# One packing product placed earlier, and h's tiles moved to one place modulo 512 bytes

## The chip, the core and the metric

The kernel runs on one core of a Trainium2 chip. The core has a matrix engine (TensorE, PE in the profile), a vector engine (VectorE, DVE), a scalar engine (ScalarE, ACT), GpSimd (POOL) and a queue for transfers (SyncE, SP). Data lies in SBUF, 128 partitions wide; PE writes its results to PSUM, in eight buffers of 2 KB a partition. A matmul on PE has two instructions: a load of the stationary operand (PEld in the profile) and the matmul that streams the moving operand.

The metric is the time of one execution on the device, in microseconds.

## What is computed

Eight batches, each with eight heads, 576 positions and a head size of 64, go through a two-step attention over 32 "pack" queries; all outputs, 4608 rows of 512, go through a gated feed-forward layer.

```
scale = 1.0 / np.sqrt(64)
def sm_attn(qq, kk, vv):
    s = scale * qq @ kk.T
    a = exp(s - max(s))
    a = a / (sum(a) + 1e-09)
    return a @ vv
p_packed = sm_attn(p, k, v)               # 32 rows a head
x = sm_attn(q, p_packed, p_packed)        # 576 rows a head
x = x.transpose(0, 2, 1, 3).reshape(4608, 512)
g = x @ w_gate                            # 512 x 1536
out = (silu(g) * (x @ w_val)) @ w_out     # 1536 x 512
```

## The kernel before

The kernel never forms x. For each batch it multiplies the packed values into the gate and value weights (the **middle product**, tiles mh and ml, `m_mm`, L570 to L588), so that the gate and value matmuls take the second attention's weights a2 directly. Operands of the large matmuls are split into a high and a low part (mh and ml, a2h and a2l, hh and hl, wo_h and wo_l), of which three products are summed.

Batch 0 and the loading of the weights follow a list of words written out by hand (PROGRAM, L41). Batches 1 to 7 run through `batch` (L903): a loop over twelve chunks `fc` of 128 hidden columns. Each chunk has two halves, A (256 positions) and B (320). Each half does

- `gv_chunk` (L623): twelve matmuls, six for the gate and six for the value, into two PSUM buffers named gv (two exist, used in turns); ACT takes silu of the gate into sg (L644), DVE multiplies it with the value into hf (L648) and, in half B, a rest into t (L651);
- `h_split` (L614): ACT writes hh, the high part of hf (L177), DVE writes hl, the rest (L618);
- six matmuls of the chunk before (`out_mm`, L654): the stationary operand is hl or hh, the moving one is wo_h or wo_l, the sum goes to one of four PSUM buffers named acc.

So on PE the halves alternate: gate and value matmuls of this half, then the output matmuls of the chunk before.

The attention of the next batches is done in pieces between these matmuls. Two tables, FIRST (for batch 2) and LATER (for the later ones), give each piece a place: `4.ha turn1` is chunk 4 of the batch before, half A, at the point between the writing of hh and that of hl; `hb` is the same point of half B, `a` and `b` the points just behind silu, and numbers count the points in the matmuls. What is issued at such a point stands in each engine's program there, and each engine works its own program in order. Here the pieces of interest are

- `turn0`, `turn1` (`q_turn`, L459): for half of the heads each, DVE scales the exponentials e by the factors and transposes them into a (L464, L467);
- `pack` (`q_pack`, L471): 80 small matmuls with a as the stationary and the values v_t as the moving operand, into one gv buffer (L479), then a transpose by DVE into ppt (L485). Each small matmul is in float32 and appears as two matmuls and two loads in the profile: 160 and 160. This is called the packing product below.

In LATER, the second transpose stands at `4.ha`, the packing product at `5.ha`. In chunk 5, half A, the middle product of chunk 6 (L266, eight matmuls in the program, 16 in the profile) comes directly ahead of it.

Tiles come from pools that give each name a fixed number of buffers in turns, laid one behind the other in SBUF. The tiles hh and hl (`h_tile`, L608) have three buffers of 280 elements of four bytes; of these, 256 are used, starting at an element that changes with each use:

```
n = places[t] = places.get(t, -1) + 1
at = (0, 1, 2, 4, 8, 12, 16, 20)[n % 8]
return pool.tile([P, 280], F32R, tag=t, bufs=3, name=t)[:, at : at + 256]
```

The middle product's tiles mh and ml are shifted in the same way (L576). All of w_out's tiles start at the same byte modulo 512 of a partition.

Of the kernel before, what the change touches and what calls it, by code (L numbers as in the profile page):

```python
# [10 lines left out]
F32 = mybir.dt.float32  # L11
F32R = mybir.dt.float32r
# [8 lines left out]
B, H, S, D = 8, 8, 576, 64  # L21
NP = 32
DM, DF = 512, 1536
P = 128
NPAR, NHP = 2, 4
NFC = DF // P
NSC = -(-S // P)
NJ, SQ = 4, S // 4
# [7 lines left out]
F64_HI_LEAST = float(np.array(897 << 20, np.int32).view(np.float32))  # L36
F64_HI_MOST = float(np.array(0x47EFFFFF, np.int32).view(np.float32))
SPLIT = 5
LOW_WORD = -(2.0**-51) * 15 / 16

PROGRAM = """  # L41
# [23 lines left out]
FIRST = """  # L65
# [33 lines left out]
LATER = """  # L99
# [32 lines left out]
def tile_pack_attention_swiglu(ctx: ExitStack, tc: tile.TileContext, qT, kT, v, vq, pT, wgv, wout, out):  # L132
# [5 lines left out]
    pool = ctx.enter_context(tc.tile_pool(name="pool", bufs=1))  # L138
# [51 lines left out]
    def f64_convert(dst, st, shape):  # L190
# [5 lines left out]
        yield nc.scalar.activation(dst, hi.bitcast(F32), AF.Abs)  # L196
        yield nc.scalar.activation(lo.bitcast(F32), lo.bitcast(U32), AF.Identity, bias=minus_two, scale=LOW_WORD)
        yield nc.vector.tensor_scalar(dst, dst, F64_HI_LEAST, F64_HI_MOST, op0=ALU.max, op1=ALU.min)
# [11 lines left out]
    def pair(dtype, name):  # L210

        return pool.tile([P, 2, DM], dtype, tag="pair", bufs=NFC + 1, name=name)
# [11 lines left out]
    def wout_high(fc):  # L224
        k, i = divmod(fc, 2)
        if i == 0:
            wo_h[k], wo_l[k] = pair(F32R, "wo_h"), pair(F32R, "wo_l")
        pin(nc.scalar.copy(wo_h[k][:, i], wos[k][:, i]))
# [126 lines left out]
        nc.vector.reciprocal(rs[:, 2], rs[:, 1])  # L355

    def s1_scale(b):
        pp = pool.tile([P, NPAR, D], F32, tag="pp", bufs=1, name="pp")
        nc.vector.tensor_tensor(
            pp,  # L360
            pps[b][0][:, : NPAR * D].rearrange("p (r d) -> p r d", r=NPAR),
            st1[b][2][:, 2].unsqueeze(2).broadcast_to([P, NPAR, D]),
            op=ALU.mult,
        )
        pps[b].append(pp)
# [57 lines left out]

    def q_gather(b):

        x = pool.tile([P, NJ, 2, H], F32, tag="x1", bufs=1, name="x1")
        zd = dram.tile([P, 2, H], F32, tag="zd", bufs=2, name="zd")
        nc.sync.dma_start(zd, sq[b][1].rearrange("p s r h -> p s (r h)"))
        for i in range(NJ):
            nc.sync.dma_start(x[NP * i : NP * i + NP], zd.rearrange("(j n) s h -> n j s h", j=NJ))  # L430
        sq[b].append(x)
# [168 lines left out]
    def m_part(b, k, fcs):  # L600
        m_mm(b, k, fcs)
        m_high(b, k, fcs)

    t4 = {}

    places = {}

    def h_tile(t):  # L608

        n = places[t] = places.get(t, -1) + 1  # L610
        at = (0, 1, 2, 4, 8, 12, 16, 20)[n % 8]
        return pool.tile([P, 280], F32R, tag=t, bufs=3, name=t)[:, at : at + 256]

    def h_split(src, hi, lo, between=lambda: False, tag=""):  # L614
        hh, hl = (pool.tile([P, 256], F32R, tag=t + tag, bufs=2, name=t) if tag else h_tile(t) for t in ("hh", "hl"))
        copy(hi, hh, src)
        last = between()
        low = lo.tensor_tensor(hl, src, hh.bitcast(F32), op=ALU.subtract)  # L618
        if last:
            pin(low)  # L620
        return hh, hl
# [32 lines left out]
    def out_mm(acc, hh, hl, c, fc):  # L654
        for i, (h_, w_) in enumerate(((hl, wo_h), (hh, wo_l), (hh, wo_h))):
            nc.tensor.matmul(  # L656
                acc[:, :],
                h_[:, c : c + P],
                w_[fc // 2][:, fc % 2],
                start=(fc == 0 and i == 0),  # L660
                stop=(fc == NFC - 1 and i == 2),
            )

    def emit_out(acc, row, eng):
# [13 lines left out]
        "q1r": lambda d: q_read(d, 1, (0, 1)),  # L678
        "q1e": lambda d: q_exp(d, 1),
        "q1z": lambda d: (q_sums(d, 1), q_gather(d)),  # L680
        "common": q_common,
        "common_e": q_common_exp,
# [10 lines left out]
    for i in range(2):  # L693
        for name, f in (
# [8 lines left out]
        ):  # L703
            words2[f"{name}{i}"] = (lambda f, i: lambda d: f(d, (d + i) % 2))(f, i)

    def plan_of(b):

        plan = {}
        for d in (b + 1, b + 2):
            if d >= B:  # L710
                continue
            for line in (FIRST if d == 2 else LATER).strip().splitlines():
                place, *todo = line.split()
                fc, place = place.split(".")
                fc = int(fc) + NFC * (d - b - 1)
                if (0 if d > 2 else -NFC) <= fc < NFC:
                    plan.setdefault((fc, int(place) if place.isdigit() else place), []).extend((words2[w], d) for w in todo)
        return lambda fc, place: bool([f(d) for f, d in plan.pop((fc, place), ())])

    with tc.manual_schedule(engines={mybir.EngineType.PE}):  # L720
# [17 lines left out]
        with tc.manual_schedule(  # L738
# [25 lines left out]

            h0 = [pair(F32, "h0") for _ in range(SPLIT)]
            for k in (*range(NFC // 2 - 2), NFC // 2 - 1, NFC // 2 - 2):
# [24 lines left out]
            def half(i):  # L791
                fc, is_b = order[i]
                if fc // 2 < SPLIT:
                    return h0[fc // 2][:, fc % 2, 256 * is_b : 256 * is_b + 256]
# [18 lines left out]
            def h_high(i):  # L813
                hs[i].append(h_tile("hh"))
                nc.scalar.copy(hs[i][1], hs[i][0])

            def h_low(i):
                hs[i].append(h_tile("hl"))
                nc.vector.tensor_tensor(hs[i][2], hs[i][0], hs[i][1].bitcast(F32), op=ALU.subtract)

            def outs(i):
                fc, is_b = order[i]
                for c in range(2):
                    if fc // 2 >= SPLIT:
                        out_mm(accs[2 * is_b + c], *hs[i][1:], c * P, fc)
# [29 lines left out]
            def half_of(f, b):  # L855
# [9 lines left out]
                "z_top": lambda x: s1_top(0), "z_exp": lambda x: s1_exp(0, True), "z_turn": lambda x: s1_turn(0, x),  # L865
                "z_turned": lambda x: s1_turned(0, x, nc.vector), "z_pack": lambda x: s1_pack(0),
                "z_sums": lambda x: s1_sums(0, True), "z_scale": lambda x: s1_scale(0), "z_flip": lambda x: s1_flip(0),
                "z_ppt": lambda x: s1_ppt(0), "two_mm": lambda c: (None if c else s2_tiles(0), s2_mm(0, c)),
                "two_block": lambda c: s2_block(0, c), "narrow": narrow, "heat": warm_up,
# [5 lines left out]
                "s1_keep": lambda x: s1_keep(1, x), "s1_top": lambda x: s1_top(1), "s1_exp": lambda x: s1_exp(1),  # L875
                "s1_turn": lambda x: s1_turn(1, x), "s1_turned": lambda x: s1_turned(1, x, nc.scalar),
                "s1_pack": lambda x: s1_pack(1), "s1_sums": lambda x: (s1_sums(1), s1_scale(1)),
                "s1_flip": lambda x: s1_flip(1), "s1_ppt": lambda x: s1_ppt(1),
                "s2_mm": two_mm, "s2_block": lambda x: s2_block(1, x), "s2_max": half_of(s2_max, 1),
# [7 lines left out]
            for word in PROGRAM.split():  # L887
                name = word[: word.index(":") + 1] if ":" in word else word.rstrip("0123456789")
# [14 lines left out]
        def batch(b, behind):  # L903
            if not b % 2:
                t4_of(b)
            run = plan_of(b)
            ha, hb = {}, {}
            accs, rows = [], []
# [7 lines left out]
            for fc in range(NFC):  # L916
                count = [0]

                def fill():
                    count[0] += 1  # L920
                    if count[0] == 2:
# [3 lines left out]
                        elif fc % 2 and fc + 1 < NFC:  # L925
                            m_part(b, (fc + 1) // 2, both)
                    if b == 1 and 1 <= fc <= 2 * SPLIT - 4 and count[0] == 7:
                        wout_high(fc + 3)
# [91 lines left out]
```

## Time and profile before

| | us |
|---|---|
| runs shown | 738.66, 741.58, 741.37 |
| their median | 741.37 |
| the profiled execution | 741.01 |
| its span, first to last instruction | 739.2 |
| PE busy in it | 727.5 |
| DVE busy | 454.3 |
| ACT busy | 373.7 |

The profile is one execution with times of every instruction. Its page sums them by engine and by line; a timeline lists them in order (start, duration, engine, line, operation, output and inputs, count, and in brackets the idle time ahead of it and what ended that); windows give the busy time of each engine between two times, with the clock that the matrix engine was granted (1.00 is full speed) and the share of the transfer engines in use. "issue" is waiting that nothing in the profile explains. A matmul's duration overlaps the next one's, so the pace is read from the starts. Queues named "instruction" carry the engines' own programs.

### The profile page before, as it was taken

The numbers are of one execution on the slowest core, as the hardware profiler recorded it, in microseconds if no ns is written. First come the engines' busy times: TensorE is split into PE (matmuls) and PEld (weight loads), VectorE is DVE, ScalarE is ACT, GpSimd is POOL, SyncE is SP. The second block draws the span as 40 slices with busy tenths as digits, with TensorE's granted clock in tenths as the row PEclk, the third lists the DMA queues.
The fourth block names the chain that finished last, engine by engine and source line by source line (L and its number), as shares of the span: only waits on it lengthen the run. The fifth ranks groups of instructions, "written<-read, shape, count | busy, mean of one in ns | idle before, by whom it ended". The sixth has DMA issues, their size and how long they took to land.

```text
span 739.2 us, 15099 instructions
## 1 busy us (share of the span) xinstructions
PE 727.5 (98%) x6242; PEld 593.4 (80%) x6242; DVE 454.3 (61%) x1009; ACT 373.7 (51%) x668; POOL 2.0 (0%) x13
## 2 busy tenths in 40 slices
PE   7899999999999999999999999999999999999997
PEld 4656667888888888888888778888888888888886
DVE  5999879665755557564665537655574555644333
ACT  3788647755535355552654525654453535533331
POOL 0000000000000000000000000000000000000000
PEclk9999999999999999999999999999999999999999
DMA  9797482320112201302112021012001000010001
GB/s 348 269 341 276 144 311 94 100 73 1 65 65 77 74 1 66 125 4 73 65 58 83 4 73 65 30 31 73 1 2 69 7 2 1 1 58 1 1 1 71
DMA packets 20004, 59.15 MB, mean 80 GB/s; under 512 B 5984, under 2 KB 7008, under 8 KB 17376
## 3 DMA queue, kind: packets, MB, share of 16 engines
q1 hardware_dynamic: 19792, 58.12, 21.8%
q8 instruction: 49, 0.80, 0.5%
q14 instruction: 19, 0.16, 0.1%
q10 hardware_dynamic: 144, 0.07, 0.0%
HBM read 48.69 MB, written 9.49 MB: 79 GB/s over the span
## 4 chain that ended last, share of the span: by engine, by line
PE 95%; DVE 1%; issue 0%; DVEq 0%
PE gv L637 36%; PE acc L656 34%; PE aux L266 7%; PE gv L786 5%; PE acc L827 5%; PE aux L656 5%; PE gv_aux L479 1%; PE gv_aux L395 1%; PE gv_aux L266 1%; DVE w L199 0%; PE acc L727 0%; PE aux L342 0%; DVE w L200 0%; PE aux L323 0%; DVE ot L179 0%
## 5 line engine op out<-in xcount | busy, mean ns | idle before, releaser
L644 ACT ACTIVATE sg<-gv 128x256 f32<-128x256 f32 (+1 forms) x168 | 69.0, 411 | 180.4 <-PE gv L637 166.6
L648 DVE TENSOR_TENSOR hf<-gv,sg 128x256 f32<-128x256 f32 x168 | 71.0, 422 | 131.6 <-PE gv L637 120.0
L637 PE MATMUL gv<-a2h,ml 128*128 128x256 f32 (+1 forms) x672 | 144.7, 297 | 0.0
L637 PE MATMUL gv<-a2l,mh 128*128 128x256 f32 (+1 forms) x672 | 144.1, 296 | 0.0
L637 PE MATMUL gv<-a2h,mh 128*128 128x256 f32 (+1 forms) x672 | 143.8, 295 | 0.0
L656 PE MATMUL acc<-wo_h,hl 128*128 128x512 f32 x344 | 140.6, 409 | 0.0
L656 PE MATMUL acc<-wo_h,hh 128*128 128x512 f32 x344 | 136.1, 395 | 0.0
L656 PE MATMUL acc<-wo_l,hh 128*128 128x512 f32 x344 | 135.9, 395 | 0.0
L637 PEld LDWEIGHTS gv<-a2h,ml 128*128 128x128 f32 x672 | 117.1, 189 | 15.8 <-ACT sg L802 0.4
L177 ACT CAST hh<-hf 128x256 fp32r<-128x256 f32 x168 | 67.8, 403 | 102.4 <-DVE hf L648 102.3
L637 PEld LDWEIGHTS gv<-a2l,mh 128*128 128x128 f32 x672 | 108.4, 189 | 0.0
L637 PEld LDWEIGHTS gv<-a2h,mh 128*128 128x128 f32 x672 | 108.0, 189 | 0.0
L618 DVE TENSOR_TENSOR hl<-hf,hh 128x256 fp32r<-128x256 f32 x168 | 70.0, 416 | 46.3 <-ACT hh L177 46.2
L656 PEld LDWEIGHTS acc<-wo_h,hl 128*128 128x128 f32 x344 | 64.6, 188 | 26.9 <-issue 18.3
L656 PEld LDWEIGHTS acc<-wo_h,hh 128*128 128x128 f32 x344 | 64.8, 189 | 15.1
L656 PEld LDWEIGHTS acc<-wo_l,hh 128*128 128x128 f32 x344 | 64.8, 188 | 8.1 <-issue 0.2
L566 DVE TENSOR_TENSOR ml<-aux,mh 128x512 fp32r<-128x512 f32 x92 | 59.0, 682 | 5.2 <-ACT mh L596 5.1
L266 PE MATMUL aux<-w,ppt 64*32 64x512 f32 (+1 forms) x784 | 52.1, 588 | 0.9 <-DVE w L200 0.9
L596 ACT CAST mh<-aux 128x512 fp32r<-128x512 f32 x92 | 49.4, 590 | 5.6 <-PE aux L266 1.3
L644 ACT ACT_TABLE_LOAD x30 | 38.5, 1283 | 13.8 <-PE gv L637 10.0
L827 PE MATMUL acc<-wo_f,h 128*128 128x512 f32 x80 | 37.8, 603 | 0.0
L827 PEld LDWEIGHTS acc<-wo_f,h 128*128 128x128 f32 x80 | 14.2, 190 | 16.6 <-issue 16.2
(153 smaller groups left out, 754.8 us busy)
## 6 DMA issues: line engine op xcount, KB each, us to landing
st<-in_wgv SPq DMA_DIRECT2D x12, 1024.0 KB, 6.4
k_t<-in_kT SPq DMA_DIRECT2D x16, 576.0 KB, 5.0
q_t<-in_qT SPq DMA_DIRECT2D x16, 576.0 KB, 4.9
out<-ot SPq DMA_DIRECT2D x36, 256.0 KB, 2.1
v_t<-in_vq SPq DMA_DIRECT2D x6, 1280.0 KB, 5.9
st<-in_wout SPq DMA_DIRECT2D x6, 1024.0 KB, 6.4
v_t<-in_v SPq DMA_DIRECT2D x2, 1024.0 KB, 8.6
p_t<-in_pT SPq DMA_DIRECT2D x7, 64.0 KB, 2.5
```

The lines of the kernel that those rows point to most:

```text
L177: e.copy(dst, src)
L266: nc.tensor.matmul(outs[par][32 * hp : 32 * hp + 32], lhs(r, hp), rhs(r, hp), start=True, stop=True)
L395: nc.tensor.matmul(pss[par][NP * j : NP * j + NP, i * SQ : (i + 1) * SQ], p_t[r, 2 * g + i, :], k_t[r, j // 2, 2 * g + i, j % 2 * SQ : j % ...
L566: pin(nc.vector.tensor_tensor(*lows.pop(0), op=ALU.subtract))
L596: nc.scalar.copy(m[0][at], src)
L618: low = lo.tensor_tensor(hl, src, hh.bitcast(F32), op=ALU.subtract)
L637: nc.tensor.matmul(pg[:, :n], m_[:, g, f, s * P : (s + 1) * P], a_[:, g, off : off + n], start=(i == 0), stop=(i == 5),)
L644: nc.scalar.activation(sg[:, :n], pgs[0][:, :n], AF.Silu)
L648: nc.vector.tensor_tensor(hf, pgs[1][:, o : o + 256], sg[:, o : o + 256], op=ALU.mult)
L656: nc.tensor.matmul(acc[:, :], h_[:, c : c + P], w_[fc // 2][:, fc % 2], start=(fc == 0 and i == 0), stop=(fc == NFC - 1 and i == 2),)
L786: nc.tensor.matmul(held[i][s][:, :n], m_[:, g, f, s * P : (s + 1) * P], a_[:, g, off : off + n], start=(j == 0), stop=(j == len(todo) - 1),)
L827: nc.tensor.matmul(accs[2 * is_b + c], half(i)[:, c * P : c * P + P], wos[fc // 2][:, fc % 2], start=(fc == 0), stop=(fc == NFC - 1),)
```

## The change

Two things change.

First, `pack` of batch 5 moves from `5.ha` to `4.hb`, one half chunk and one group of output matmuls earlier; the other batches keep their place. On PE (batch 4, chunk 4, half B, then chunk 5, half A), before, the 320-column gate and value matmuls are followed by output matmuls:

```order
L637 MATMUL gv<-a2h,ml 128x320 x2
L637 MATMUL gv<-a2l,mh 128x320 x2
L637 MATMUL gv<-a2h,mh 128x320 x2
L656 MATMUL acc<-wo_h,hl 128x512
L656 MATMUL acc<-wo_l,hh 128x512
L656 MATMUL acc<-wo_h,hh 128x512
```

and the packing product (L479) stands some way behind them, after the 256-column matmuls and the middle product (L266):

```order
L637 MATMUL gv<-a2l,mh 128x256 x2
L637 MATMUL gv<-a2h,mh 128x256 x2
L266 MATMUL aux<-w_84,ppt 32x512 x8
L479 MATMUL gv_aux<-v_t,a_4713 32x32 x80
L656 MATMUL acc<-wo_h,hl 128x512
L656 MATMUL acc<-wo_l,hh 128x512
L656 MATMUL acc<-wo_h,hh 128x512
```

Now, at the first of these places, with what each instruction waits for in brackets (lines are three higher here, those of the h tiles two lower):

```order
L635 MATMUL gv<-a2l,mh 128x320 x2
L635 MATMUL gv<-a2h,mh 128x320 x2
L482 MATMUL gv_aux<-v_t,a_4713 32x32 [waits DMAHW6_49,Activation_49]
L482 MATMUL gv_aux<-v_t,a_4713 32x32
L482 MATMUL gv_aux<-v_t,a_4713 32x32 [waits DVE_49]
L482 MATMUL gv_aux<-v_t,a_4713 32x32 x77
L654 MATMUL acc<-wo_h,hl 128x512
L654 MATMUL acc<-wo_l,hh 128x512
```

The product has moved ahead of six output matmuls, twelve gate and value matmuls and the middle product. Its first matmul waits for a transfer and for ACT, as before; its third has a wait for DVE that it did not have. On DVE at the same place, before, the transpose of the result (ppt) stands behind the multiplication (hf) of the next half, with a_4713 the transposed exponentials of batch 5:

```order
L467 STREAM_TRANSPOSE a_4713<-e_4263 128x640
L618 TENSOR_TENSOR hl<-hf,hh 128x256
L648 TENSOR_TENSOR hf<-gv,sg 128x256
L651 TENSOR_TENSOR t_4360<-gv,sg 128x64
L618 TENSOR_TENSOR hl<-hf,hh 128x256
L648 TENSOR_TENSOR hf<-gv,sg 128x256
L485 STREAM_TRANSPOSE ppt<-gv_aux 128x128
L618 TENSOR_TENSOR hl<-hf,hh 128x256
```

and now:

```order
L470 STREAM_TRANSPOSE a_4713<-e_4263 128x640
L616 TENSOR_TENSOR hl<-hf,hh 128x256
L646 TENSOR_TENSOR hf<-gv,sg 128x256
L649 TENSOR_TENSOR t_4360<-gv,sg 128x64
L488 STREAM_TRANSPOSE ppt<-gv_aux 128x128
L616 TENSOR_TENSOR hl<-hf,hh 128x256
L646 TENSOR_TENSOR hf<-gv,sg 128x256
L616 TENSOR_TENSOR hl<-hf,hh 128x256
```

The transpose of the result stands ahead of one writing of hl and one of hf. The programs of ACT, GpSimd and the transfer queue are the same as before.

Second, the tiles hh and hl lose their shifts and their 24 spare elements: three buffers of 1024 bytes each, always used from the start. Two paddings, 120 elements behind pp and six rows more in x1, move what lies behind them so that every hh and hl tile starts at 448 modulo 512 bytes, while w_out's tiles start at 192. No instruction is added or removed.

```diff
+PAD = 120
@@ s1_scale
-        pp = pool.tile([P, NPAR, D], F32, tag="pp", bufs=1, name="pp")
+        pp = pool.tile([P, NPAR * D + PAD], F32, tag="pp", bufs=1, name="pp")[:, : NPAR * D].rearrange(
+            "p (r d) -> p r d", r=NPAR
+        )
@@ q_gather
-        x = pool.tile([P, NJ, 2, H], F32, tag="x1", bufs=1, name="x1")
+        x = pool.tile([P, NJ + 6, 2, H], F32, tag="x1", bufs=1, name="x1")[:, :NJ]
@@
-    places = {}
-
     def h_tile(t):
-
-        n = places[t] = places.get(t, -1) + 1
-        at = (0, 1, 2, 4, 8, 12, 16, 20)[n % 8]
-        return pool.tile([P, 280], F32R, tag=t, bufs=3, name=t)[:, at : at + 256]
+        return pool.tile([P, 256], F32R, tag=t, bufs=3, name=t)
@@
+    def table_of(d):
+        return FIRST if d == 2 else LATER.replace("5.ha pack", "4.hb pack") if d == 5 else LATER
+
@@ plan_of
-            for line in (FIRST if d == 2 else LATER).strip().splitlines():
+            for line in table_of(d).strip().splitlines():
```

## The prediction

> **What bounds the kernel now.** The page's first part and its chain of work come first.
>
> ```profile
> PE 727.5 (98%) x6242; PEld 593.4 (80%) x6242; DVE 454.3 (61%) x1009; ACT 373.7 (51%) x668; POOL 2.0 (0%) x13
> PE 95%; DVE 1%; issue 0%; DVEq 0%
> ```
>
> PE is the bound: 98% busy, 95% of the chain that ended last. DVE and ACT have room, so a change counts only where it alters what PE does, or when PE may start. I therefore took PE's timeline next, at the place the change names, the packing product (L479) that batch 4 issues for batch 5.
>
> ```profile
> 421.45 1.09 PE L266 MATMUL aux<-w,ppt 64*32 64x512 f32 x16
> 422.46 1.48 PE L479 MATMUL gv_aux<-v_t,a 128*32 128x32 f32 x150
> 426.24 0.31 PE L479 MATMUL gv_aux<-v_t,a 128*32 128x32 f32 x10 [2.30 <-issue]
> 426.49 0.50 PE L656 MATMUL acc<-wo_h,hl 128*128 128x512 f32 x1
> ...
> 428.36 0.73 PE L637 MATMUL gv<-a2h,ml 128*128 128x320 f32 x2
> ...
> 431.28 0.39 PE L656 MATMUL acc<-wo_h,hl 128*128 128x512 f32 x1
> ```
>
> PE stops for 2.30 us in the middle of a product, after 150 of its 160 matmuls, waiting for no engine and no transfer of data ("issue"). The same stretch, from a product's start through the outputs and the 320-column gate and value matmuls behind it, can be cut out for all six such products by windows:
>
> ```profile
> core 0: us, PE busy (x) PEld busy (x) DVE busy (x) ACT busy (x) POOL busy (x), PEclk, DMA share, GB/s
> 158.18:162.91 4.73, 4.73 (x186) 4.43 (x179) 2.17 (x6) 1.82 (x4) 0.00 (x0) 1.00 0.43 138
> 248.97:253.82 4.85, 4.85 (x186) 4.55 (x179) 1.82 (x4) 1.53 (x4) 0.00 (x0) 1.00 0.45 147
> 331.52:336.25 4.73, 4.73 (x186) 4.43 (x179) 1.82 (x4) 1.53 (x4) 0.00 (x0) 1.00 0.46 133
> 422.46:431.28 8.81, 6.51 (x186) 6.01 (x179) 1.82 (x4) 1.53 (x4) 0.00 (x0) 0.81 0.42 148
> 509.00:513.83 4.83, 4.83 (x186) 4.53 (x179) 1.82 (x4) 1.53 (x4) 0.00 (x0) 1.00 0.44 139
> 599.90:604.62 4.73, 4.73 (x186) 4.43 (x179) 1.82 (x4) 1.53 (x4) 0.00 (x0) 1.00 0.02 3
> ```
>
> Same instructions, but 8.81 us for batch 5's against 4.73 for three of the others. **4.08 us are lost here**, more than the pause, because the granted clock is low behind it:
>
> ```profile
> 426.50:428.40 1.90, 1.90 (x11) 1.54 (x8) 1.80 (x4) 0.00 (x0) 0.00 (x0) 0.76 0.45 89
> 428.40:431.30 2.90, 2.90 (x14) 2.90 (x13) 0.02 (x1) 0.44 (x1) 0.00 (x0) 0.57 0.94 385
> 431.30:435.20 3.90, 3.90 (x24) 3.46 (x24) 1.41 (x4) 1.16 (x3) 0.00 (x0) 1.00 0.03 11
> ```
>
> **What PE waits for.** The page's queues and the queues between 422.4 and 423.9 us answer it (one digit of the second row is 0.0375 us):
>
> ```profile
> q8 instruction: 49, 0.80, 0.5%
> DMA  0000000000000000000000000000009000000000
> q8 instruction: 1, 0.02, 5.2%
> ```
>
> Queue q8 carries PE's own program: 6242 matmuls and 6242 weight loads in 49 transfers, 255 instructions and 0.80 MB / 49 = 16 KB each, so blocks of 256. In the stall's window one block is fetched, at 423.53 us (the 31st digit). The missing instruction is the product's 301st (150 matmuls with their loads are 300), so the last block PE had began at its 45th. A product drains 320 instructions in 1.5 us, while 256 instructions last 15 us on average (739.2 / 12484 x 256). From the fetch's start at 423.53 to PE's going on at 426.24 are 2.7 us; that is the time a block must be asked for ahead.
>
> Counting PE's program in blocks of 256 from that point, the borders fall in the six products at 103, 231, 173, 45 and 301, 243, and 115. Only the fourth needs two new blocks within itself. Borders at 231 and 243 cost 0.12 and 0.10 us in the windows, borders at 103, 115 and 173 nothing.
>
> **The change part by part.** The product moves ahead of six output matmuls (12 instructions with their loads), twelve gate and value matmuls (24), the middle product of 16 matmuls (32) and one semaphore instruction: 69. The program's length is the same, so the borders stand still and batch 5's product has them at 114 and, 370, 49 instructions behind its end. The sixth product (115, 371) and the first (103, 359) are its twins, both 4.73 us. The block at 370 is asked for about when PE crosses 114; in the stall the fetch began 1.07 us behind the product's start with the border at 45, here some 0.3 us later, plus 2.7: there at 4.1 us. PE needs it after the product (1.49), six outputs (1.48), twelve matmuls (1.50) and 13 of 32 instructions (0.4): at 4.9 us. So the stall goes and nothing takes its place in this stream: **-4.08 us**.
>
> What is late next at the new place is read from these rows; the product follows the 320-column matmuls that end at 418.54:
>
> ```profile
> 417.91 0.44 ACT L644 ACTIVATE sg<-gv 128x320 f32<-128x320 f32 x1 [0.15 <-PE gv L637]
> 418.02 0.84 DVE L467 STREAM_TRANSPOSE a<-e 128x640 f32<-128x640 f32 x1
> 418.24 0.46 PE L637 MATMUL gv<-a2h,mh 128*128 128x320 f32 x2
> 418.54 0.39 PE L656 MATMUL acc<-wo_h,hl 128*128 128x512 f32 x1
> 420.88 0.40 PE L637 MATMUL gv<-a2l,mh 128*128 128x256 f32 x2
> 421.11 0.40 PE L637 MATMUL gv<-a2h,mh 128*128 128x256 f32 x2
> L479 PEld LDWEIGHTS gv_aux<-v_t,a x960: 105/109/114, 158.2 to 601.2; 128*32 128x32 f32 x192
> ```
>
> - A wait is added: the product's third matmul reads the half of a that DVE's second transpose writes, and that ends at 418.86. Without it PE would be there at about 418.6. With the hand-over and a load (0.11) it goes on at about 419.0: **+0.40 us**, between 0 (the transpose lies on DVE, and any earlier end frees it) and 0.8 (that much again if DVE is later). Behind the waiting matmul stand all of PE's work; on DVE the transpose of the result now stands ahead of hl of the same chunk, which is read only behind the next 320-column matmuls, some 7 us on (1.49 + 1.50 + 1.0 + 1.5 + 1.75). The PSUM buffer it takes is free: its reader, ACT's silu, ends at 418.35.
> - Entering 32-column matmuls from gate and value ones costs PE a step: 421.11 to 421.45 is 0.34 for two matmuls that take 0.23 in the row above: **+0.10**.
> - Outputs behind such a product are slower than behind gate and value matmuls. Here the old group loses its cheap start:
>
> ```profile
> 331.52 1.56 PE L479 MATMUL gv_aux<-v_t,a 128*32 128x32 f32 x160
> 333.01 0.50 PE L656 MATMUL acc<-wo_h,hl 128*128 128x512 f32 x1
> ...
> 334.50 0.45 PE L637 MATMUL gv<-a2h,ml 128*128 128x320 f32 x2
> ```
>
>   333.01 to 334.50 is 1.49; the group at 418.54 takes 1.40 (below): **+0.08**. The later group keeps such a start, behind the middle product (1.49 to 1.50, below): 0 to +0.01.
>
> **The addresses.** In the built programs w_out's tiles lie at 192 modulo 512. Before, hh starts at 480, 64 or 160 and hl at 256, 352 or 448, plus 0 to 80 bytes by turns; after, all start at 448, 256 away from w_out. The padding keeps gate and value pairs at their old distances: ml, mh and a2 all move by 32. No instruction is added; only PE's pace could change. The windows of six output matmuls (the first three behind 32-column work, the others behind gate and value) and of twelve gate and value ones:
>
> ```profile
> 346.63:348.15 1.52, 1.52 (x6) 1.05 (x6) 1.00 0.00 0
> 360.29:361.79 1.50, 1.50 (x6) 1.04 (x6) 1.00 0.15 18
> 409.32:410.81 1.49, 1.49 (x6) 1.05 (x6) 1.00 0.05 4
> 402.24:403.63 1.39, 1.39 (x6) 0.95 (x6) 1.00 0.00 0
> 418.54:419.94 1.40, 1.40 (x6) 0.94 (x6) 1.00 0.00 0
> 381.42:382.82 1.40, 1.40 (x12) 1.37 (x11) 1.00 0.84 312
> 337.64:339.06 1.42, 1.42 (x12) 1.38 (x11) 1.00 0.19 79
> L656 PE MATMUL acc<-wo_h,hl 128*128 128x512 f32 x344 | 140.6, 409 | 0.0
> L656 PE MATMUL acc<-wo_h,hh 128*128 128x512 f32 x344 | 136.1, 395 | 0.0
> ```
>
> At 346.63 hl lies at 448, the new place, and the group takes 0.025 us more than the two below it. At 381.42 ml lies 256 (and 0) from a2, and that group is no slower than at 337.64, with other distances. The pace thus hardly follows the place. With 344 matmuls of each of the three terms, 172 groups: a loss of 0.025 each would be +4.3 us, a gain of 0.01 (1.49 for 1.50, 1.39 for 1.40) -1.7. I take **0**, to which the gate and value rows are nearest, and keep -1.7 and +4.3. ACT's and DVE's writes to the moved tiles have the two engines' idle time as cover.
>
> **Sum**: -4.08 + 0.40 + 0.10 + 0.08 = -3.50 us. The profiled execution took 741.01 us (span 739.2): **737.5 us**. The median shown, 741.37, lies 0.36 above it; the run of 738.66 may have had a shorter stall, which no trace shows.
>
> **A rule of the skill.** The low clock starts about a microsecond behind a pause of 2.30 us. The Trainium skill, TensorE: Matmul & The Clock Gate, Part 1, says that the clock is halved after an idle window of about 3.4 us, and warns of gaps over about 3 us. By that rule the pause is too short, and the slow stretch behind it has another cause that need not go. The five other windows, same work and up to the same DMA share, have clock 1.00, so here the trace goes against the rule.
>
> **Rivals.**
> - *The slow clock stays.* Something other than the pause halves it. The pause was 4.02 - 1.49 = 2.5 of the 4.08 (422.46 to 426.49 against 331.52 to 333.01), so 1.55 stay: 739.1. Against it stand the five windows at 1.00. It is also what the Trainium skill's rule above would give.
> - *The stall stays.* The 2.30 us are not the block's fetch, or the fetch stalls at 370 too; then only the added costs remain: 741.0 + 0.58 = 741.6. Against it: the twins, and 0.8 us of margin.
> - *Place costs a little.* Only hl's reads suffer, as at 346.63: 737.5 + 4.3 = 741.8.
> - *Place costs at every read: slower.* At 346.63 two reads of six are 256 away. If they make the 0.025, each is 0.0125, and all 1032 output matmuls pay: +12.9, 750.4. It makes the kernel slower from 3.4 ns a matmul on (3.50 / 1032). Against it: 381.42.
>
> **How the numbers follow.** Forecast 0.68, its own range 735.8 to 739.2; clock stays 0.06; stall stays 0.08; hl alone 0.07; every read 0.11. The range runs from the gain (737.5 - 1.7, less 1.0 for differences between executions) to hl's loss: 734.8 to 741.8; it leaves out every read and a little below. A measurement here tells about 0.5%, 3.7 us, so the forecast stands almost on the border at 737.7: of its 0.68, 0.42 count as faster and 0.26 as within. With the three middle rivals within: faster 0.42, same 0.47, slower 0.11.
>
> **What would show it.** Right: batch 5's product as one row of x160 near 418.6, no "issue" in it, a short wait of its first matmuls on DVE's L470, clock 1.00 up to 435 us, the output rows' means at 409 and 395 ns as now. Wrong: a pause of over 1 us anywhere between 418 and 428, a clock below 1.00 without one, or output groups that all take 1.42 or more behind gate and value matmuls.

## The result, and the profile after

The changed kernel takes 735.3 us (median of 6 runs, 735.01 to 736.46) against 741.07 (6 runs, 738.66 to 741.58): a ratio of 0.9937, with a 95% interval of 0.992 to 0.9953. The forecast was 737.5, the range 734.8 to 741.8. The profiled execution after took 736.46 us, its span 734.7; it is the slowest of its six. It also has 3.4 us of half clock at 12 us, in the start, for which the mean clocks of the other five, 0.999 to 1.000 against its 0.998, leave no room.

The page after, PE and the chain:

```profile
PE 725.7 (99%) x6242; PEld 592.0 (81%) x6242; DVE 454.4 (62%) x1009; ACT 373.9 (51%) x668; POOL 2.0 (0%) x13
PE 95%; DVE 1%; issue 0%; DVEq 0%
```

PE is still the bound, with the same 6242 matmuls. PE's timeline after, at the place the change names (start, duration, line, operation, output and inputs, count):

```profile
418.38 0.45 PE L635 MATMUL gv<-a2h,mh 128*128 128x320 f32 x2
418.76 1.83 PE L482 MATMUL gv_aux<-v_t,a 128*32 128x32 f32 x160
420.52 0.50 PE L654 MATMUL acc<-wo_h,hl 128*128 128x512 f32 x1
...
422.01 0.40 PE L635 MATMUL gv<-a2h,ml 128*128 128x256 f32 x2
...
423.52 1.09 PE L267 MATMUL aux<-w,ppt 64*32 64x512 f32 x16
424.54 0.50 PE L654 MATMUL acc<-wo_h,hl 128*128 128x512 f32 x1
```

The product is one row of x160, and no row has "issue" in it. From its start to the outputs are 1.76 us; an undisturbed one has 1.49, so it waits 0.27. The wait is on DVE, as forecast: DVE's second transpose ends at 418.16 + 0.84 = 419.00, while PE is there at 418.76, and the loads (PEld) name it as what they waited for.

```profile
418.16 0.84 DVE L470 STREAM_TRANSPOSE a<-e 128x640 f32<-128x640 f32 x1
419.06 1.42 PEld L482 LDWEIGHTS gv_aux<-v_t,a 128*32 128x32 f32 x156 [0.15 <-DVE a L470]
```

The windows after, over batch 5's product and the two runs of matmuls behind it and, for comparison, the same over batch 4's and batch 6's (behind these the gate and value matmuls have 320 columns, behind batch 5's now 256):

```profile
331.99:336.72 4.73, 4.73 (x186) 4.43 (x179) 1.82 (x4) 1.53 (x4) 0.00 (x0) 1.00 0.45 136
418.76:423.52 4.76, 4.72 (x179) 4.17 (x178) 1.64 (x6) 0.79 (x2) 0.00 (x0) 1.00 0.43 124
505.32:510.05 4.73, 4.73 (x186) 4.43 (x179) 1.82 (x4) 1.53 (x4) 0.00 (x0) 1.00 0.45 146
```

Clock 1.00 in all of them: the pause and the slow stretch of before are both gone. The output matmuls changed too. By the rows of before and after for the two kinds of output, the usual ones (acc) and those of the 128 rows that two batches share (aux, the **tail** below, 144 matmuls with the tiles hh4 and hl4):

```profile
L656 PE MATMUL acc<-wo_l,hh 128*128 128x512 f32 x344 | 135.9, 395 | 0.0
L656 PE MATMUL aux<-wo_l,hh 128*128 128x512 f32 x48 | 19.0, 395 | 0.0
```

```profile
L654 PE MATMUL acc<-wo_h,hl 128*128 128x512 f32 x344 | 140.7, 409 | 0.0
L654 PE MATMUL acc<-wo_h,hh 128*128 128x512 f32 x344 | 135.4, 394 | 0.0
L654 PE MATMUL acc<-wo_l,hh 128*128 128x512 f32 x344 | 134.8, 392 | 0.0
L654 PE MATMUL aux<-wo_l,hh 128*128 128x512 f32 x48 | 18.7, 389 | 0.0
```

The rows at 395 are shorter, in the tail by 6 ns; the one at 409 is not. Durations overlap, so the pace is in the starts. The last output matmuls of the tail before, then after:

```profile
731.79 0.39 PE L656 MATMUL aux<-wo_h,hl 128*128 128x512 f32 x1
...
735.06 0.39 PE L656 MATMUL aux<-wo_h,hh 128*128 128x512 f32 x1
```

```profile
728.02 0.39 PE L654 MATMUL aux<-wo_h,hl 128*128 128x512 f32 x1
...
730.51 0.39 PE L654 MATMUL aux<-wo_h,hh 128*128 128x512 f32 x1
```

14 steps take 3.27 us before (234 ns each), 11 take 2.49 after (226). Over all starts in the trace, from each output matmul to the next matmul, the tail's step is 233.1 ns before and 227.6 after (143 steps, -0.79 us), and within the groups of six output matmuls 232.3 and 231.4 (824 steps under 260 ns, -0.68 us). So besides the pause about 1.5 us came in these steps from the tiles' places, for which the forecast had 0.

### The profile page after: what moved, and what is told of

It is laid out like the page before. It is cut to its first block, busy times and chain, and to the rows that moved or that the text cites. A ratio compares the mean times of both kernels' runs of the same rounds, so it can differ in the third digit from the quotient of the medians.

```text
span 734.7 us, 15099 instructions
## 1 busy us (share of the span) xinstructions
PE 725.7 (99%) x6242; PEld 592.0 (81%) x6242; DVE 454.4 (62%) x1009; ACT 373.9 (51%) x668; POOL 2.0 (0%) x13
## 4 chain that ended last, share of the span: by engine, by line
PE 95%; DVE 1%; issue 0%; DVEq 0%
PE gv L635 36%; PE acc L654 33%; PE aux L267 7%; PE gv L787 6%; PE acc L828 5%; PE aux L654 4%; PE gv_aux L482 1%; PE gv_aux L398 1%; PE gv_aux L267 1%; DVE w L200 0%; PE acc L728 0%; PE aux L343 0%; DVE e L467 0%; DVE w L201 0%; PE aux L324 0%
```

## The experiments

The first four kernels separate the two parts and move the tiles' place. In what follows, ratios are to the kernel before on the same chip.

**The product alone.** `plan_of` as changed, h's tiles and the paddings as before.

```diff
-        return pool.tile([P, 256], F32R, tag=t, bufs=3, name=t)
+        at = (0, 1, 2, 4, 8, 12, 16, 20)[n % 8]
+        return pool.tile([P, 280], F32R, tag=t, bufs=3, name=t)[:, at : at + 256]
```

> Batch 5's packing product earlier, h's tiles as before. Block theory (the pause is the fetch of PE's next block of 256 instructions, the slow clock follows from the pause): no pause, clock 1.00 around 420 us, 741.1 - 3.7 = about 737.4 us, output matmuls at the pace of before (409, 395, 395 ns; groups of six behind gate and value matmuls 1.39 us on average). Rival, the whole gain is the stall: 735.3 us, as with both parts. Rival, the slow clock has another cause: pause gone but a stretch with half clock still within some us, 739.

737.6 us (737.02 to 738.53), ratio 0.996 (0.9944 to 0.9976). The pause is gone, clock 1.00 from 417 to 434 us, steps of 232.2 and 233.1 ns as before. The added costs can be read without the tiles:

```profile
417.96 0.45 PE L637 MATMUL gv<-a2h,mh 128*128 128x320 f32 x2
418.34 1.82 PE L479 MATMUL gv_aux<-v_t,a 128*32 128x32 f32 x160
420.09 0.50 PE L656 MATMUL acc<-wo_h,hl 128*128 128x512 f32 x1
...
421.60 0.40 PE L637 MATMUL gv<-a2h,ml 128*128 128x256 f32 x2
```

The product takes 1.75, the outputs behind it 1.51, and the last two gate and value matmuls 0.38 in place of 0.30. The first theory holds; that the stall is the whole gain does not.

**The tiles alone.**

```diff
-        return FIRST if d == 2 else LATER.replace("5.ha pack", "4.hb pack") if d == 5 else LATER
+        return FIRST if d == 2 else LATER
```

> h's tiles at 448 modulo 512 without shifts, the packing product where it was. If the two parts add up: the pause of 2.3 us and the half clock behind it are there as before, output matmuls about 8 ns a group of six faster and the last output groups of each pair (tiles hh4 and hl4) some 5 ns a matmul faster, 741.1 - 1.7 = about 739.4 us. Rival, the tiles do nothing: 741.1 us. Rival, the tiles matter only through where the product lands: not under 741.

738.26 us (737.04 to 739.59), ratio 0.9968 (0.9956 to 0.9981), steps of 231.3 and 227.6 ns as after. The parts add up: 0.996 x 0.9968 = 0.9928 against 0.9937 for both. But one expectation failed. The pause is there, and in this execution no half clock follows it:

```profile
422.30 1.48 PE L482 MATMUL gv_aux<-v_t,a 128*32 128x32 f32 x150
425.88 0.31 PE L482 MATMUL gv_aux<-v_t,a 128*32 128x32 f32 x10 [2.10 <-issue]
...
427.61 0.46 PE L635 MATMUL gv<-a2h,ml 128*128 128x320 f32 x2
```

```profile
423.00:426.00 3.00, 0.90 (x102) 0.79 (x89) 0.00 (x0) 0.53 (x2) 0.00 (x0) 1.00 0.03 5
426.00:429.00 3.00, 3.00 (x26) 2.70 (x24) 1.82 (x4) 0.25 (x1) 0.00 (x0) 1.00 0.61 190
429.00:432.00 3.00, 3.00 (x21) 2.74 (x20) 0.98 (x3) 0.89 (x3) 0.00 (x0) 1.00 0.60 253
```

The slow stretch is thus not certain to follow. Of the executions without a profile only the mean clock is on record, and it does not tell where the clock was low: in this profile it is 0.995 because of 6.8 us of half clock at 12 us, in the start, and two of the six runs with the product alone, whose profile has no pause, have 0.994 and 0.995. Of the 17 runs of the kernel before that were made beside these, five have 0.999 or 1.000, which leaves no room for a slow stretch, and take 738.79 to 739.6 us; twelve have 0.998 or less and take 740.33 to 742.39. So at most twelve had half clock behind the pause. The spread of the runs of before goes with half clock, there or in the start.

**The same place as w_out's, and a quarter away.** PAD of 56 elements puts h's tiles at 192 modulo 512, distance 0 from w_out; PAD of 88 at 320, distance 128.

```diff
-PAD = 120
+PAD = 56
```

> Both parts, but the padding is 56 elements in place of 120: h's tiles at 192 modulo 512, the same as w_out's, distance 0 in place of 256; gate and value pairs keep their distances. Theory that the distance of 256 makes the output matmuls' pace: the gain of 1.6 us is lost or more, 737 us or above, output groups of six behind gate and value matmuls over 1.39 us. Rival, any fixed place without shifts does it: 735.3 us and the same group times.

> Both parts, padding of 88 elements: h's tiles at 320 modulo 512, 128 from w_out's. Distance theory, with 256 as the best place: between the place of 256 (735.3) and the spread places of before (737). Rival, any fixed place without shifts does it: 735.3 us.

Distance 0: 735.34 us (734.9 to 736.76), ratio 0.993 (0.9914 to 0.9946), steps as with 256. So 256 is no better than 0. Distance 128: 736.52 us (735.58 to 737.32), ratio 0.9944 (0.9928 to 0.9959), steps of 231.3 ns in the groups and 232.1 in the tail. The rival, any fixed place, does not hold for the tail.

The next three test the theory of the blocks by moving the borders and the products apart from each other.

**The borders moved, the products not.** Tiles as changed, all products at their old places, 17 of the 34 warm-up matmuls left out of PROGRAM (every second `heat` or `warm` word); their result is used nowhere.

```diff
-    load_k0 load_w0 heat2 heat1 heat2 load_v0 heat2 load_q0 z_scores0 heat1 z_max0 z_scores1 heat1 z_max1 z_top
+    load_k0 load_w0 heat1 load_v0 heat2 load_q0 z_scores0 z_max0 z_scores1 heat1 z_max1 z_top
...
```

> h's tiles as changed, every packing product at its place of before, but 17 of the 34 warm-up matmuls in the first 80 us are left out (they feed nothing), so PE's program is 68 instructions shorter ahead of all products. Block theory: the borders of the blocks of 256 fall 68 instructions later in each product: batch 5's at 113, no pause there; batch 3's at 43 and 299, a pause of about 2.3 us after 149 of its 160 matmuls; batch 6's at 55 and 311, a pause of about 2.3 us after 155 of 160. Rival, the pause belongs to batch 5's product or to what runs at 423 us: one pause, in batch 5's product.

The timeline, at batch 3's, batch 5's and batch 6's product:

```profile
249.36 1.46 PE L482 MATMUL gv_aux<-v_t,a 128*32 128x32 f32 x149
251.90 0.32 PE L482 MATMUL gv_aux<-v_t,a 128*32 128x32 f32 x11 [1.07 <-issue]
...
423.72 1.56 PE L482 MATMUL gv_aux<-v_t,a 128*32 128x32 f32 x160
...
506.06 1.51 PE L482 MATMUL gv_aux<-v_t,a 128*32 128x32 f32 x155
509.95 0.26 PE L482 MATMUL gv_aux<-v_t,a 128*32 128x32 f32 x5 [2.38 <-issue]
```

The pauses stand after 149 and 155 matmuls, as counted, and batch 5's has none. The one of 2.3 us forecast for batch 3 was 1.07: in the trace its block's transfer begins at 249.55, 0.19 us behind the product's start, while that of the stall before began 1.07 behind. Why it began earlier is open. Behind the longer pause the clock is halved, behind the shorter not:

```profile
249.30:254.20 4.90, 3.83 (x178) 3.33 (x171) 1.82 (x4) 1.16 (x3) 0.00 (x0) 1.00 0.24 53
510.40:513.80 3.40, 3.40 (x11) 2.83 (x11) 1.68 (x4) 0.00 (x0) 0.00 (x0) 0.50 0.80 249
```

The time, 741.3 us, ratio 1.0007 (0.9993 to 1.0021), also has the missing warm-up in it; its profile has half clock in the start too, for 3.4 us at 12 and at 26 us.

**The same move for batch 3.** On the changed kernel:

```diff
-... if d == 5 else LATER
+... if d in (3, 5) else LATER
```

> The changed kernel, with batch 3's packing product moved to 4.hb as well. Block theory: its borders go from -26 and 230 to 43 and 299, as batch 5's were before the change, so it gets a pause of about 2.3 us after 149 matmuls; the half clock may or may not follow. 735.3 + 2.5 + 0.4 = 738.2 us without it, up to 739.8 with it. Rival, the earlier place is better by itself: 735.3 us or less.

```profile
244.98 1.73 PE L482 MATMUL gv_aux<-v_t,a 128*32 128x32 f32 x149
248.83 0.32 PE L482 MATMUL gv_aux<-v_t,a 128*32 128x32 f32 x11 [2.12 <-issue]
```

The pause comes to a product that had none, after the 149 matmuls counted, and the time lies where it was expected: 739.72 us (737.64 to 740.26), ratio 0.9983 (0.9971 to 0.9995), 4.4 more than with batch 5's alone. The earlier place is worth nothing by itself.

**Batch 5's product 12 instructions later**, behind the output matmuls:

```diff
-LATER.replace("5.ha pack", "4.hb pack")
+LATER.replace("5.ha pack", "4.8 pack")
```

> The changed kernel, with batch 5's packing product behind the output matmuls (4.8) in place of ahead of them (4.hb): 12 instructions later, borders at 101 and 357, and 36 instructions behind the product in place of 48 until the next border. Block theory with the times of the first trace: the block is there 4.3 us behind the product's start and needed after 3.4, a pause of about 0.9 us in the middle product behind the gate and value matmuls; in exchange no wait for DVE (0.3 us). 735.3 + 0.6 = 735.9 us. Rival, the margin is larger: no pause, 735.0 us.

```profile
422.22 2.08 PE L267 MATMUL aux<-w,ppt 64*32 64x512 f32 x16
424.23 0.50 PE L654 MATMUL acc<-wo_h,hl 128*128 128x512 f32 x1
```

The middle product takes 2.01 us from start to start; after the change it takes 1.02 (423.52 to 424.54). That is a pause of 0.99, where 0.9 was expected, in the place expected. 736.61 us (735.76 to 737.19), ratio 0.9948 (0.993 to 0.9967), is 1.3 above the change where 0.6 was expected; the rest is not accounted for. Here "issue" is not shown, since the matmuls' modelled ends cover the gap; only the starts tell.

The last five ask what it is in the tiles' places.

**No shifts in mh and ml either**, with a padding of 216 elements: mh, a2h and a2l at 192, ml and h's tiles at 448.

```diff
-            at = (0, 1, 2, 4, 8, 16)[k]
-                pool.tile([P, NPAR * 4 * P + 24], dt, ...)[:, at : at + NPAR * 4 * P].rearrange(
+                pool.tile([P, NPAR * 4 * P], dt, ...).rearrange(
```

> The changed kernel, with mh and ml without shifts and spare elements as well, all of mh, a2h and a2l at 192 and ml at 448 modulo 512. Theory that the shifts, not the distance, cost pace: gate and value matmuls 0.4% faster as the output matmuls were, 271.1 us of them become 270.0, 734.2 us. Rival, only a gain for 512-column matmuls: 735.3 us. Rival, the shifts of mh and ml gain something: above 736 us.

736.74 us (736.2 to 737.01), ratio 0.9948 (0.9931 to 0.9964). The gate and value matmuls take 134.9 ns from start to start against 134.3 to 134.5 with their shifts (where the trace has no half clock in them), 2016 of them, so the step went the wrong way: what helps the output matmuls does not help these. That is the last rival's forecast, though the run changes the places of these tiles along with their shifts.

**h's tiles spread over their old places but without shifts; and three more common places.**

```diff
-        at = (0, 1, 2, 4, 8, 12, 16, 20)[n % 8]
+        at = 0
```

> Batch 5's product earlier, h's tiles of 1120 bytes at their three and three places of before (480, 64, 160 and 256, 352, 448 modulo 512), but always used from the start. Theory that the shifted views cost pace: matmuls within a group of six from 232.2 ns to 231.4, 736.5 us. Rival, one common place for all tiles is what counts: 232.2 ns as in the kernel with the product alone moved, 737.4 us. The tail's tiles (hh4, hl4) are as before in both: 233.1 ns.

> The changed kernel with a padding of 128 elements: one common place, 480 modulo 512, 288 from w_out's, a multiple of 32 and not of 64 bytes. Theory that one common place is what counts: 231.4 ns within a group. Rival, starts at multiples of 64 bytes count: 232.2 ns or above. The tail's tiles then lie at 480 too: 227.6 ns if only the spread counted there, about 233 if the distance does.

> The changed kernel with a padding of 8 elements: h's tiles at 0 modulo 512, 320 from w_out's, that is 64 modulo 256; a start at a multiple of 64 bytes. Theory that starts at multiples of 64 bytes make the pace: 231.4 ns within a group, as at 192, 320 and 448, and 736.5 us or less. Rival, the distance from w_out's place modulo 256 makes it, with 0 the best: over 231.8 ns within a group, and 232 to 233 ns in the tail, 737 us or above.

> The changed kernel with a padding of 104 elements: h's tiles at 384 modulo 512, 192 from w_out's. Theory of multiples of 64 bytes: 231.4 ns within a group, 736.5 us or less. Rival, the distance modulo 256: over 231.8 ns within a group, 232 to 233 ns in the tail, 737 us or above.

The four ratios are 0.9962 (0.995 to 0.9973) for the spread, 0.9964 (0.9952 to 0.9976) for place 480, 0.9955 (0.994 to 0.997) for 0 and 0.9938 (0.9921 to 0.9954) for 384. Place 0 was made with a padding of 8 elements; 136 give the same place, but need 0.03 KB a partition more than SBUF has left. The starts of all output matmuls in each trace give one table. All these kernels have batch 5's product at 4.hb. The distance is from w_out's place modulo 512.

| h's place | distance | step in groups, ns | step in the tail, ns | median, us |
|---|---|---|---|---|
| spread, shifted | mixed | 232.2 | 233.1 | 737.6 |
| spread, not shifted | mixed | 232.3 | 233.1 | 737.5 |
| 448 (the change) | 256 | 231.4 | 227.6 | 735.3 |
| 192 | 0 | 231.4 | 227.6 | 735.3 |
| 320 | 128 | 231.3 | 232.1 | 736.5 |
| 384 | 192 | 230.9 | 231.5 | 736.0 |
| 480 | 288 | 232.6 | 233.3 | 737.6 |
| 0 | 320 | 232.6 | 233.3 | 737.6 |

Three theories fall. It is not the shifts (second row), not a common place (480 and 0 are no better than the spread), and not starts at multiples of 64 bytes (0 is one). For the tail the first two rows are one case, not mixed: hh4 and hl4 have no shifts in any of these kernels (L615), and in these two programs they lie at 160, distance 480.

What agrees with the tail is the distance modulo 256: 0 is the best, 128 and 192 lie between, 32, 64 and 224 are no gain. The groups follow it in part: 0, 128 and 192 differ by 0.5 ns at most, and 192 is the fastest. For 384 the distance theory had expected over 231.8 ns and 737 us or above, and missed; multiples of 64 had expected 231.4 or so, and only place 0 speaks against them. Nor is the distance shown to be the cause: w_out lay at 192 in all of these kernels, so the place of h's tiles modulo 256, taken alone, fits the rows as well. Why, and why the gate and value matmuls do not follow it, is open.

## Why the prediction was right, and where it was off

- **What PE waits for.** Shown. The pause was taken out of batch 5's product and put into batch 3's and batch 6's by moving the product or the borders of the 256-instruction blocks, to the matmul: 149, 155 and 149 were counted, and found. Its length was less sure: of three forecast at about 2.3 us, one was 1.07.
- **The pause goes and nothing takes its place.** Right. The 12 instructions fewer between product and border brought 0.99 us of pause back (0.9 worked out). But the margin of 0.8 us was not there, and it is partly luck that no pause came. The text had the block's fetch begin about 1.4 us behind the product's start; the queues between 420.3 and 421.0 us (one digit is 0.0175 us) put it at 420.96, 2.20 behind:

```profile
DMA  0000000000000000000000000000000000000090
q8 instruction: 1, 0.02, 8.6%
```

  PE needed the block in the middle product that begins at 423.52, 2.6 us after the fetch began. In the traces with a pause, PE went on 2.35 to 2.87 us after it (2.71 in the stall before).
- **-4.08 us.** Too large for a median. The term holds 2.5 us of pause and 1.55 of half clock, and the second is not in every run of before (at most twelve of 17). The product alone brought 740.73 - 737.6 = 3.1 us, with 3.50 forecast. Among runs with a mean clock of 0.999 or 1.000 it brought 739.39 - 737.36 = 2.0 us (medians of five and of four), and 2.5 less the added 0.58 is 1.9.
- **+0.40 for the wait on DVE.** Right in its place; it was 0.27. The transpose ended 0.24 us behind PE's arrival, and the next load began 0.06 us after that (419.06), where 0.14 was thought.
- **+0.10 and +0.08 for the changes of shape.** Right: 418.38 to 418.76 is 0.38 for a pair that took 0.30, so 0.08, and 420.52 to 422.01 is 1.49 for a group that took 1.40, so 0.09.
- **0 for the places.** This term was mis-sized, and both rivals on the places had the wrong sign. The steps counted above give -1.5 us; those from output matmuls into gate and value ones and back give another -0.34 against the product alone. The medians give more, 735.3 - 737.6 = -2.3 us (-2.0 at place 192 on the same chip, among runs at 0.999 or 1.000), which is beyond the -1.7 that the text kept as its end; the rest is not accounted for. So the time fell below the forecast's own range (735.8 to 739.2) and is inside the wide one by the 1.0 us taken off there for differences between executions. Two things led the term astray. It took the gate and value rows as the nearest evidence, and those do not behave like the output matmuls. And it counted 172 groups but not the tail's 144 matmuls, which gave half of the 1.5. The group at 346.63, which seemed to speak against the distance of 256, was slow for a reason that no run here settles.
- **The rival by the Trainium skill**, TensorE: Matmul & The Clock Gate, Part 1, that the clock is halved after an idle window of about 3.4 us, which no pause here fills: not borne out. Pauses of 2.12 to 2.38 us were followed by half clock in the profiles of before, of the moved borders and of batch 3's move; one of 2.10, with the tiles alone, was not, nor the 1.07. The Trainium skill says there too that the window runs freely. The slow stretch of 3.4 us (clock 0.50 over 510.40 to 513.80) has the window's length. A window that is only partly idle might be enough, and chance then decide; no run here tests this.

Of what the text named as marks of being right, all came but "means as now": the 409 stayed, the 395 fell by 1 to 3 ns.

## What to carry to other kernels

A burst of very small matmuls can outrun the supply of PE's own program, and whether it does is decided by where a border of 256 instructions falls in it: a pause with "issue" as its releaser, in one of several equal stretches, is to be compared with the instruction queue before any data dependency is blamed. Any edit ahead of such a burst, even leaving out a warm-up matmul, moves the borders and can make a pause come or go some hundred microseconds later, so a small gain or loss of such an edit needs a look there first. The place of a matmul's operands in SBUF is worth a trial, 0.3 per cent here between the best and the worst, and one kind of matmul did not tell about the other.

## What the runs showed that was not expected

- The pace of 128x512 output matmuls changes with the place of h's tiles modulo 256 bytes, w_out's being fixed: 227.6 to 233.3 ns a step in the tail, with no change in any instruction.
- Half clock followed three of four pauses of 2.1 to 2.4 us, and cost about 1.5 us in the one where it was worked out. It did not follow a pause of 1.07.
- The time from the fetch of a block to PE going on was 2.35 to 2.87 us in the traces with a pause, and the fetch began 0.2 to 1.4 us behind the start of the product that then stalled.
